# Attention, experts and a gated layer on one core: the order of the last layer's gate passes and weight passes

## The chip, the cores and the metric

One NeuronCore of a Trainium2 chip runs the whole program in one launch. The metric is device time in microseconds, the median of three runs. The output is float32.

## What is computed

Three layers follow each other on 2304 tokens of 512 values.

```python
p_packed = sm_attn(p, k, v)               # 4 batches, 8 heads, 576 tokens, 32 packed queries
x = sm_attn(q, p_packed, p_packed)        # softmax attention, both times
for e in range(4):                        # experts, 512 -> 1024 -> 512, weighted by domain_probs
    out += p[:, e:e + 1] * (np.maximum(x @ w1[e], 0.0) @ w2[e])
h = out @ w_in                            # the last layer, 512 -> 2048
r = np.maximum(h, 0.0)
g = s * (r * r) + b                       # the gate
return g @ w_out                          # 2048 -> 512
```

The change touches only the last layer.

## The kernel before

Every product of the last layer runs on TensorE with each operand split in a high part (rounded for the engine's fast float32 form) and a low part (what the rounding left): three matmuls stand for one. A split is two passes: ACT copies the high part, and DVE (POOL for w_out) subtracts it from the source.

The layer's width of 2048 is cut in four groups g of 512 (NG = 4), the tokens in three pairs tp of two blocks of 384 (T3 = 384, NTP = 3). A **tile** is one (g, tp). Inside a tile both products are 2 x 2 block products done with seven multiplications in place of eight, named 11, 12, s2, s3, s1, s4, 22 (OPS); the s are sums of blocks. A tile's first product is 7 operations k times 2 column blocks j, so 14 **steps** (UP = 14) of six 384-column matmuls (L1053, `m3_mm`). `m3_next` takes the results from PSUM: operations 11, s2, s3 and 22 accumulate in one bank per j ("a"), which is read after each of them, 12, s1 and s4 take a bank of their own ("b"). ACT copies (L1110, L1118, L1112), DVE adds (L1119), and four quarters of h come out: z0 with 12, z3 with s3, z1 with s4, z2 with 22. ORDER says in which order the seven are done.

From group 1 on the gate is five short functions, put on steps by a table (`at(step, fn, ...)`, in the loop over g near the end; `pos` turns a unit of the last layer into a step): `q_relu` (ACT, L1128), `q_gate` (ACT, a square L1133 and a scale with bias L1135), `q_sum` (DVE, the sums s1 to s4 of the gated quarters, L1147) and `q_part` (the split: high pass on ACT L1156, low pass on DVE L1159). The quarters are called 11, 12 for the upper and 21, 22 for the lower values; the upper are z0 and z1 of j = 0, 1, the lower z2 and z3.

The second product (L1191, `m4_next`) has seven operations again, in the order LAST, of 18 matmuls of 256 columns: three row blocks i of 128 tokens with six each. It lags by 18 steps, nine matmuls behind each step's six (`second`). Rows 0 and 2 of an operation share a PSUM bank (o0 or o2, by b), the middle row 1 sits in bank o1, whose two halves serve the operations in turn. After row 1, and again after row 2, DVE adds the bank to the output in SBUF (L1206); TensorE may write a bank again only after that addition has read it. In the last group the finished rows go out by DMA from SP.

Beside a tile, the next group's operands are made. `wop_parts` splits w_in's operand for operation k (ACT L789, DVE L790, two column blocks each), a step apart, during the last tile (tp = 2) of the group before; `wi_sums` (POOL, L774 to L781) forms the block sums in place, `wov_parts` does w_out's (ACT L831, POOL L832) from step 6 of a group's first tile. Operands of x come back from DRAM by SP's DMAs (`xs_load`).

Each engine runs its own queue in order; what stands in front and waits holds everything behind it.

Of the kernel before, what the change touches and what calls it, by code (L numbers as in the profile page):

```python
# [19 lines left out]
def attention_experts_mlp_kernel(  # L20
# [675 lines left out]
    ORDER = ("11", "12", "s2", "s1", "s3", "s4", "22")  # L696
    LAST = ("12", "11", "s2", "s1", "s3", "s4", "22")
# [85 lines left out]
    def wop_parts(g, k):  # L783
        n = g * NK + k
        tag = "w1" if n % 8 < 4 else "w1p"
        t = wop[g, k] = keep.tile([P, NQ, 2, HK * P], F32R, tag=tag, bufs=4, name=f"wop{g}{k}")
        for j in range(NQ):
            src = tw[g * NQ + j][(ORDER if g else OPS)[k]]
            nc.scalar.activation(t[:, j, 0], src, AF.Copy)  # L789
            nc.vector.tensor_tensor(out=t[:, j, 1], in0=src, in1=f32(t[:, j, 0]), op=ALU.subtract)  # L790
# [21 lines left out]
    def wov_sums(g, n):  # L812
# [8 lines left out]
        else:  # L821
            t = tv[g]
            t2, t4 = t["s2"], t["22"] = t["11"], t["12"]
            nc.gpsimd.tensor_tensor(out=t2, in0=t["s4"], in1=t["s1"], op=ALU.subtract)
            nc.gpsimd.tensor_tensor(out=t4, in0=t4, in1=t2, op=ALU.subtract)
# [311 lines left out]
    def q_sum(g, tp, what):  # L1137
# [3 lines left out]
            "s3": ("11", "21", ALU.subtract, "21"), "s4": ("12", "s2", ALU.subtract, "12"),  # L1141
# [39 lines left out]
    def m4_next(g, tp, k, i, n):  # L1181
# [4 lines left out]
        if (bank, "next") not in o_ps:  # L1186
# [7 lines left out]
            start=(n == 0 and i < 2 and (op in ("11", "12") or (op, i) == ("s1", 0))),  # L1194
# [12 lines left out]
        if g == NG - 1 and op in ("s4", "22"):  # L1207
            for j in (1,) if i == 1 else (0, 2):
                r0 = t * T3 + j * P
                nc.sync.dma_start(out=out[r0 : r0 + P], in_=o_sb[t][:, j])  # L1210


    with tc.manual_schedule():
# [291 lines left out]
        for g in range(1, NG):  # L1505
# [4 lines left out]
            for k in range(NK):  # L1510
                at(u0 + 2 * k + 1, wop_parts, g, k)
# [9 lines left out]
            for tp in range(NTP):  # L1521
                i = pos((g * NTP + tp) * UP)
                for j in range(NQ):
                    for d, n in ((3, 0), (9, 3), (11, 1)):
                        at(i + d + j, q_relu, g, tp, j, n)
                    for c in range(2):
                        for n in range(2):
                            at(i + 11 + 2 * c + j + n, q_gate, g, tp, f"{c + 1}{j + 1}", n)
                for n in range(2):
                    for k in range(2):  # L1530
                        at(i + 13 + n, q_part, g, tp, k, n)
                for d, what in ((16, "s1"), (16, "s2"), (18, "s3"), (19, "s4")):
                    at(i + d, q_sum, g, tp, what)
                for k in range(2, NK):
                    for n in range(2):
                        at(i + 13 + 2 * k + n, q_part, g, tp, k, n)
# [45 lines left out]
        def behind(g, tp, *_):  # L1582
            if g == 0:
# [5 lines left out]
                for k in range(NK) for x in range(NS) for n in range(6)  # L1589
# [60 lines left out]
```

## Time and profile before

| what | value |
|---|---|
| median of three runs | 1069.21 us (1068.4 to 1069.44) |
| the profiled execution | 1069.46 us |
| its span (first to last instruction) | 1067.7 us |
| TensorE matmuls (PE) busy | 1046.9 us, 98% |
| VectorE (DVE) busy | 687.2 us, 64% |
| ScalarE (ACT) busy | 542.2 us, 51% |
| GpSimd (POOL) busy | 211.2 us, 20% |
| granted TensorE clock | 0.999 of full speed |

The profile is of one execution; the span is 1.8 us shorter than that execution's time. PE's busy time includes the modelled end of each matmul, so a short wait can hide in it. A row of a group tells the line of the kernel, the engine, the operation, output<-inputs, shapes and count, then the busy time and the mean, then how long the engine stood idle just before such instructions and what ended that.

### The profile page before, as it was taken

The numbers are of one execution on the slowest core, as the hardware profiler recorded it, in microseconds if no ns is written. First come the engines' busy times: TensorE is split into PE (matmuls) and PEld (weight loads), VectorE is DVE, ScalarE is ACT, GpSimd is POOL, SyncE is SP. The second block draws the span as 40 slices with busy tenths as digits, with TensorE's granted clock in tenths as the row PEclk, the third lists the DMA queues.
The fourth block names the chain that finished last, engine by engine and source line by source line (L and its number), as shares of the span: only waits on it lengthen the run. The fifth ranks groups of instructions, "written<-read, shape, count | busy, mean of one in ns | idle before, by whom it ended". The sixth has DMA issues, their size and how long they took to land.

```text
span 1067.7 us, 18211 instructions
## 1 busy us (share of the span) xinstructions
PE 1046.9 (98%) x6701; PEld 924.0 (87%) x6701; DVE 687.2 (64%) x1342; ACT 542.2 (51%) x1165; POOL 211.2 (20%) x222
## 2 busy tenths in 40 slices
PE   8999999999999999999999999999999999999996
PEld 5778888888888888888888888998899899999996
DVE  7885755565664255564365735799536787777776
ACT  3533334533442343443335756766576666766752
POOL 0630330321010321010321122113123142214000
PEclk9999999999999999999999999999999999999999
DMA  9874122986578446584856233347756565565523
GB/s 257 213 127 90 21 91 99 322 223 186 197 250 250 117 121 190 189 250 158 230 141 169 75 104 138 130 193 252 293 178 217 177 207 210 173 210 180 176 89 119
DMA packets 106899, 187.09 MB, mean 175 GB/s; under 512 B 49449, under 2 KB 63785, under 8 KB 106811
## 3 DMA queue, kind: packets, MB, share of 16 engines
q1 hardware_dynamic: 106539, 185.87, 55.9%
q8 instruction: 53, 0.87, 0.3%
q14 instruction: 35, 0.29, 0.1%
q10 hardware_dynamic: 272, 0.07, 0.0%
HBM read 131.11 MB, written 54.79 MB: 174 GB/s over the span
## 4 chain that ended last, share of the span: by engine, by line
PE 80%; ACT 8%; DVE 7%; issue 2%; DMA 2%; SPq 1%; ACTq 0%; DVEq 0%
PE acc L889 35%; PE h L843 19%; PE h L1053 10%; PE on L1191 6%; PE o L1171 5%; ACT z L1133 2%; ACT z L1135 2%; PE pp L625 2%; DVE o_sb L1206 1%; DVE gg L1159 1%; ACT gg L1156 1%; DMA v<-in_v_dram 1%; DVE z L1119 1%; ACT z L1128 1%; DVE wop L790 1%
## 5 line engine op out<-in xcount | busy, mean ns | idle before, releaser
L843 PEld LDWEIGHTS h<-a,w1p 128*128 128x128 f32 x1536 | 229.1, 188 | 26.5 <-issue 5.6
L843 PE MATMUL h<-a,w1p 128*128 128x320 f32 (+1 forms) x1536 | 248.4, 297 | 0.5 <-DVE hl L866 0.4
L866 DVE SCALAR_TENSOR_TENSOR hl<-h,hh 128x256 fp32r<-128x256 f32 x256 | 107.7, 421 | 216.9 <-ACT rest L864 111.0
L864 ACT ACTIVATE hh<-h 128x256 fp32r<-128x256 f32 x256 | 98.8, 386 | 221.5 <-PE h L843 218.6
L1053 PE MATMUL h<-xs,wop 128*128 128x384 f32 x1008 | 203.0, 337 | 0.0
L889 PE MATMUL acc<-w2l,hh 128*128 128x512 f32 x512 | 201.8, 394 | 0.0
L889 PE MATMUL acc<-w2h,hh 128*128 128x512 f32 x512 | 201.3, 393 | 0.0
L889 PE MATMUL acc<-w2h,hl 128*128 128x512 f32 x512 | 200.4, 391 | 0.0
L1053 PEld LDWEIGHTS h<-xs,wop 128*128 128x128 f32 x1008 | 173.0, 188 | 5.0
L1191 PE MATMUL on<-wov,gg 128*128 128x256 f32 x1134 | 157.2, 283 | 11.7 <-DVE o_sb L1206 11.1
L1191 PEld LDWEIGHTS on<-wov,gg 128*128 128x128 f32 x1134 | 148.6, 189 | 17.4 <-DVE o_sb L1206 15.2
L889 PEld LDWEIGHTS acc<-w2h,hl 128*128 128x128 f32 x512 | 96.2, 188 | 22.0
L889 PEld LDWEIGHTS acc<-w2l,hh 128*128 128x128 f32 x512 | 96.4, 188 | 15.0 <-DVE xt L914 0.4
L889 PEld LDWEIGHTS acc<-w2h,hh 128*128 128x128 f32 x512 | 96.3, 188 | 13.2
L1206 DVE TENSOR_TENSOR o_sb<-on,o_sb 128x256 f32<-128x256 f32 x126 | 67.3, 552 | 23.4 <-PE on L1191 22.6
L1171 PE MATMUL o<-wo,gg 128*128 128x512 f32 x216 | 57.2, 395 | 0.0
L688 POOL TENSOR_TENSOR w2l<-w2r,w2h 128x512 fp32r<-128x512 f32 x24 | 31.7, 1329 | 107.2 <-ACT w2h L685 106.4
L1159 DVE TENSOR_TENSOR gg<-z,gg 128x768 fp32r<-128x768 f32 x45 | 47.1, 1064 | 7.9 <-ACT gg L1156 7.9
L1128 ACT ACTIVATE z<-z 128x384 f32<-128x384 f32 x54 | 28.0, 521 | 37.3 <-DVE z L1119 37.1
L1171 PEld LDWEIGHTS o<-wo,gg 128*128 128x128 f32 x216 | 39.9, 188 | 5.9 <-DVE gg L1028 0.2
L633 DVE TENSOR_TENSOR w1o<-pp,w1o 128x512 fp32r<-128x512 f32 x48 | 29.8, 684 | 20.8 <-ACT w1o L632 20.8
L941 ACT ACTIVATE x<-xt 32x384 f32<-32x384 f32 x80 | 41.9, 523 | 1.3
(449 smaller groups left out, 1340.6 us busy)
## 6 DMA issues: line engine op xcount, KB each, us to landing
xs<-xs_dram SPq DMA_DIRECT2D x63, 768.0 KB, 4.2
w1p_dram<-w1o SPq DMA_DIRECT2D x48, 512.0 KB, 4.1
w1p<-w1p_dram SPq DMA_DIRECT2D x192, 128.0 KB, 4.3
xs_dram<-xs SPq DMA_DIRECT2D x21, 768.0 KB, 3.3
w1r<-in_moe_w_dram SPq DMA_DIRECT2D x12, 512.0 KB, 4.4
w2r<-in_moe_w_dram SPq DMA_DIRECT2D x24, 256.0 KB, 5.1
out_dram<-o_sb SPq DMA_DIRECT2D x18, 256.0 KB, 2.3
v<-in_v_dram SPq DMA_DIRECT2D x8, 512.0 KB, 9.1
```

The source lines that it names most:

```text
L688: nc.gpsimd.tensor_tensor(out=lo, in0=raw_t.pop((e, f)), in1=f32(hi), op=ALU.subtract)
L843: nc.tensor.matmul(t[:, : width(bi, hf)], lhsT=w1p_block(e, bi, f, gi, w), rhs=a2[bi][:, x, gi, part(bi, hf)], start=(n == 0), stop=(n == ...
L864: nc.scalar.activation(hi, src, AF.Relu)
L866: nc.vector.scalar_tensor_tensor(out=lo, in0=src, scalar=0.0, in1=f32(hi), op0=ALU.max, op1=ALU.subtract)
L889: nc.tensor.matmul(acc[j], lhsT=x, rhs=w, start=(f == 0 and n == 0), stop=(g == NF - 1 and n == 2),)
L941: nc.scalar.activation(dst[32 * q : 32 * q + 32, a], src[:, q], AF.Copy)
L1053: nc.tensor.matmul(ps, lhsT=w[:, a, col], rhs=x[:, z, m, :], start=(fresh and n == 0), stop=(n == 3 * HK - 1), skip_group_check=chain,)
L1128: nc.scalar.activation(z, z, AF.Relu)
L1159: nc.vector.tensor_tensor(out=t[:, 1], in0=src, in1=f32(t[:, 0]), op=ALU.subtract)
L1171: nc.tensor.matmul(acc, lhsT=lhsT, rhs=w, start=(f == 0 and n == 0), stop=(f == FG - 1 and n == 2),)
L1191: nc.tensor.matmul(ps[:, half], lhsT=gg[g, tp, k][:, x, r, i * P : (i + 1) * P], rhs=wov[g, k][:, w, r, :], start=(n == 0 and i < 2 and (o ...
L1206: nc.vector.tensor_tensor(out=dst, in0=src, in1=dst, op=ALU.add)
```

## The change

In the last layer, for groups 1 to 3:

- ORDER does 22 sixth and s4 seventh, so the lower values z2 and z3 are complete two steps sooner and z1 two steps later. The table moves `q_relu` of z1 by two steps and gates the lower values at steps 11 to 13, the upper at 14 to 16 (before: upper first).
- LAST begins with s1 (the sum of the two lower values), then 11, s2, s4, s3, 22, and ends with 12. Sums and splits are put on steps 14 to 28 in that order; the first split, with 12 and 11 at step 13 before, is at 15 now and each is two steps ahead of its use (before four). s4 gets a buffer of its own, since 12 is needed last. `wov_sums` stores its last block sum over s1.
- `wop_parts` issues the high pass at step 2k and the low pass at 2k + 1 (before both at 2k + 1).
- The second product does row 1 first, then 0, then 2 (before 0, 1, 2); the start flags and the output DMAs follow the new order.

```diff
--- before.py
+++ after.py
@@ -693,8 +693,8 @@
 
     OPS = ("11", "12", "s2", "s3", "s1", "s4", "22")
     NK = len(OPS)
-    ORDER = ("11", "12", "s2", "s1", "s3", "s4", "22")
-    LAST = ("12", "11", "s2", "s1", "s3", "s4", "22")
+    ORDER = ("11", "12", "s2", "s1", "s3", "22", "s4")
+    LAST = ("s1", "11", "s2", "s4", "s3", "22", "12")
     wi_dram = [dram.tile([P, 2, DM], F32, name=f"wi_dram{q}") for q in range(DFF // P // 2)]
     wo_dram = [dram.tile([P, DM], F32, name=f"wo_dram{fb}") for fb in range(DFF // P)]
 
@@ -780,14 +780,20 @@
                 nc.gpsimd.tensor_tensor(out=t2, in0=t["s4"], in1=t["s1"], op=ALU.subtract)
                 nc.gpsimd.tensor_tensor(out=t4, in0=t4, in1=t2, op=ALU.subtract)
 
-    def wop_parts(g, k):
+    def wop_parts(g, k, which=(0, 1)):
         n = g * NK + k
         tag = "w1" if n % 8 < 4 else "w1p"
-        t = wop[g, k] = keep.tile([P, NQ, 2, HK * P], F32R, tag=tag, bufs=4, name=f"wop{g}{k}")
+        if 0 in which:
+            wop[g, k] = keep.tile([P, NQ, 2, HK * P], F32R, tag=tag, bufs=4, name=f"wop{g}{k}")
+        t = wop[g, k]
         for j in range(NQ):
             src = tw[g * NQ + j][(ORDER if g else OPS)[k]]
-            nc.scalar.activation(t[:, j, 0], src, AF.Copy)
-            nc.vector.tensor_tensor(out=t[:, j, 1], in0=src, in1=f32(t[:, j, 0]), op=ALU.subtract)
+            if 0 in which:
+                nc.scalar.activation(t[:, j, 0], src, AF.Copy)
+            if 1 in which:
+                nc.vector.tensor_tensor(
+                    out=t[:, j, 1], in0=src, in1=f32(t[:, j, 0]), op=ALU.subtract
+                )
 
     def wo_tile(fb):
         t = wodd.tile([P, 2, DM], F32R, tag="w1p", bufs=FG, name=f"wo{fb}")
@@ -820,9 +826,9 @@
             tv[g] = {"11": b11, "12": b21, "s1": b12, "s3": t3, "s4": b22}
         else:
             t = tv[g]
-            t2, t4 = t["s2"], t["22"] = t["11"], t["12"]
+            t2, t4 = t["s2"], t["22"] = t["11"], t["s1"]
             nc.gpsimd.tensor_tensor(out=t2, in0=t["s4"], in1=t["s1"], op=ALU.subtract)
-            nc.gpsimd.tensor_tensor(out=t4, in0=t4, in1=t2, op=ALU.subtract)
+            nc.gpsimd.tensor_tensor(out=t4, in0=t["12"], in1=t2, op=ALU.subtract)
 
     def wov_parts(g, k):
         pool, tag = (gb, "wo") if ((g - 1) * NK + k) % 8 < 4 else (wodd, "w1p")
@@ -1138,7 +1144,7 @@
         a = quad[g, tp]
         x, y, op, dst = {
             "s1": ("21", "22", ALU.add, None), "s2": ("s1", "11", ALU.subtract, None),
-            "s3": ("11", "21", ALU.subtract, "21"), "s4": ("12", "s2", ALU.subtract, "12"),
+            "s3": ("11", "21", ALU.subtract, "21"), "s4": ("12", "s2", ALU.subtract, None),
         }[what]
         if dst is None:
             dst = wb.tile([P, HK, T3], F32, tag="sx", bufs=3, name=f"q{what}_{g}{tp}")
@@ -1191,7 +1197,7 @@
         nc.tensor.matmul(
             ps[:, half],
             lhsT=gg[g, tp, k][:, x, r, i * P : (i + 1) * P], rhs=wov[g, k][:, w, r, :],
-            start=(n == 0 and i < 2 and (op in ("11", "12") or (op, i) == ("s1", 0))),
+            start=(n == 0 and i < 2 and (op in ("s1", "12") or (op, i) == ("11", 0))),
             stop=(n == 5), skip_group_check=True,
         )
         if n < 5 or i == 0:
@@ -1204,7 +1210,7 @@
         if i == 1:
             dst = dst[:, 0]
         nc.vector.tensor_tensor(out=dst, in0=src, in1=dst, op=ALU.add)
-        if g == NG - 1 and op in ("s4", "22"):
+        if g == NG - 1 and op in ("22", "12"):
             for j in (1,) if i == 1 else (0, 2):
                 r0 = t * T3 + j * P
                 nc.sync.dma_start(out=out[r0 : r0 + P], in_=o_sb[t][:, j])
@@ -1508,7 +1514,8 @@
                 at(u0 - 5, load_wi, q)
             at(u0 - 2, wi_sums, g, 0)
             for k in range(NK):
-                at(u0 + 2 * k + 1, wop_parts, g, k)
+                for x in range(2):
+                    at(u0 + 2 * k + x, wop_parts, g, k, (x,))
                 if k == 1:
                     at(u0 + 3, wi_sums, g, 1)
                 for tp in range(NTP):
@@ -1521,19 +1528,16 @@
             for tp in range(NTP):
                 i = pos((g * NTP + tp) * UP)
                 for j in range(NQ):
-                    for d, n in ((3, 0), (9, 3), (11, 1)):
+                    for d, n in ((3, 0), (9, 3), (13, 1)):
                         at(i + d + j, q_relu, g, tp, j, n)
                     for c in range(2):
                         for n in range(2):
-                            at(i + 11 + 2 * c + j + n, q_gate, g, tp, f"{c + 1}{j + 1}", n)
-                for n in range(2):
-                    for k in range(2):
-                        at(i + 13 + n, q_part, g, tp, k, n)
-                for d, what in ((16, "s1"), (16, "s2"), (18, "s3"), (19, "s4")):
+                            at(i + 14 - 3 * c + j + n, q_gate, g, tp, f"{c + 1}{j + 1}", n)
+                for d, what in ((14, "s1"), (17, "s2"), (18, "s4"), (20, "s3")):
                     at(i + d, q_sum, g, tp, what)
-                for k in range(2, NK):
+                for k in range(NK):
                     for n in range(2):
-                        at(i + 13 + 2 * k + n, q_part, g, tp, k, n)
+                        at(i + 15 + 2 * k + n, q_part, g, tp, k, n)
 
         wb = wf = wodd = None
         stack_f = ExitStack()
@@ -1586,7 +1590,7 @@
                 ]
             return [
                 (m4_next, g, tp, k, x, n)
-                for k in range(NK) for x in range(NS) for n in range(6)
+                for k in range(NK) for x in (1, 0, 2) for n in range(6)
             ]
 
         def second(count):
```

What the table makes of DVE's queue where the tile (1, 2) ends (818 to 857 us of the trace): names end in g, tp and k, so wop26 is the operand of group 2 for operation 6, gg116 the gate operand of tile (1, 1) for operation 6, o_sb the output, on a bank of the second product. Before:

```order
L1119 TENSOR_TENSOR z120_9211<-h1250_9453,uv0_7683 128x384
L790 TENSOR_TENSOR wop25_9476<-wi4_9087,wop25_9476 128x256
L790 TENSOR_TENSOR wop25_9476<-wi5_9089,wop25_9476 128x256
L1119 TENSOR_TENSOR z121_9237<-h1251_9481,uv1_7719 128x384
L1206 TENSOR_TENSOR o_sb3_8630<-on_1_8988,o_sb3_8630 128x256
L1206 TENSOR_TENSOR o_sb3_8630<-on_2_8981,o_sb3_8630 128x2x256
L1159 TENSOR_TENSOR gg116_9470<-z111_8918,gg116_9470 128x768
L790 TENSOR_TENSOR wop26_9528<-wi4_9087,wop26_9528 128x256
L790 TENSOR_TENSOR wop26_9528<-wi5_9089,wop26_9528 128x256
L1206 TENSOR_TENSOR o_sb3_8630<-on_1_8988,o_sb3_8630 128x256
L1206 TENSOR_TENSOR o_sb3_8630<-on_0_9028,o_sb3_8630 128x2x256
```

and with the change:

```order
L1212 TENSOR_TENSOR o_sb2_8493<-on_2_8987,o_sb2_8493 128x2x256
L1165 TENSOR_TENSOR gg115_9472<-z111_8915,gg115_9472 128x768
L1125 TENSOR_TENSOR z120_9209<-h1260_9502,uv0_7683 128x384
L1212 TENSOR_TENSOR o_sb3_8630<-on_1_8979,o_sb3_8630 128x256
L794 TENSOR_TENSOR wop26_9499<-wi4_9086,wop26_9499 128x256
L794 TENSOR_TENSOR wop26_9499<-wi5_9088,wop26_9499 128x256
L1125 TENSOR_TENSOR z121_9236<-h1261_9528,uv1_7719 128x384
L1212 TENSOR_TENSOR o_sb3_8630<-on_0_9033,o_sb3_8630 128x2x256
L1165 TENSOR_TENSOR gg116_9520<-z111_8915,gg116_9520 128x768
L1153 TENSOR_TENSOR qs1_12_9549<-z120_9209,z121_9236 128x768
L1212 TENSOR_TENSOR o_sb3_8630<-on_1_8979,o_sb3_8630 128x256
```

The low passes of wop26 stood directly in front of two additions whose inputs TensorE had finished; now what stands behind them (z121, then an addition) waits for products that TensorE finishes later.

ACT's queue at the same place, which makes the high parts (wop) that those low passes wait for. Before:

```order
L1135 ACTIVATE z120_9211<-z120_9211,b_sb_80,s_sb_79 128x768
L1128 ACTIVATE z121_9237<-z121_9237 128x384
L1133 ACTIVATE z121_9237<-z121_9237 128x768
L1112 ACTIVATE z120_9211<-h1200_9212 128x384
L1133 ACTIVATE z120_9211<-z120_9211 128x768
L1135 ACTIVATE z121_9237<-z121_9237,b_sb_80,s_sb_79 128x768
L1156 ACTIVATE gg120_9522<-z121_9237 128x768
L1156 ACTIVATE gg121_9524<-z120_9211 128x768
L789 ACTIVATE wop26_9528<-wi4_9087 128x256
L789 ACTIVATE wop26_9528<-wi5_9089 128x256
```

and with the change:

```order
L1118 ACTIVATE z120_9209<-h1200_9210 128x384
L1162 ACTIVATE gg115_9472<-z111_8915 128x768
L1139 ACTIVATE z120_9209<-z120_9209 128x768
L1118 ACTIVATE z121_9236<-h1201_9237 128x384
L1141 ACTIVATE z120_9209<-z120_9209,b_sb_80,s_sb_79 128x768
L1139 ACTIVATE z121_9236<-z121_9236 128x768
L792 ACTIVATE wop26_9499<-wi4_9086 128x256
L792 ACTIVATE wop26_9499<-wi5_9088 128x256
L1162 ACTIVATE gg116_9520<-z111_8915 128x768
L1134 ACTIVATE z120_9209<-z120_9209 128x384
L1141 ACTIVATE z121_9236<-z121_9236,b_sb_80,s_sb_79 128x768
```

The two high passes of wop26 stood behind two splits of the gate (gg120, gg121) at the end of the tile; now they stand behind a square, with one split behind them.

DVE's queue in the tail, from the split of the last operation of tile (3, 1), gg316, on (qs1, qs2 and qs4 are the sums, z320 and z321 the quarters of the last tile). Before:

```order
L1159 TENSOR_TENSOR gg316_11422<-z311_10902,gg316_11422 128x768
L1206 TENSOR_TENSOR o_sb3_8630<-on_1_8988,o_sb3_8630 128x256
L1206 TENSOR_TENSOR o_sb3_8630<-on_0_9028,o_sb3_8630 128x2x256
L1159 TENSOR_TENSOR gg320_11467<-z321_11213,gg320_11467 128x768
L1159 TENSOR_TENSOR gg321_11469<-z320_11192,gg321_11469 128x768
L1206 TENSOR_TENSOR o_sb2_8490<-on_1_8988,o_sb2_8490 128x256
L1206 TENSOR_TENSOR o_sb2_8490<-on_2_8981,o_sb2_8490 128x2x256
L1147 TENSOR_TENSOR qs1_32_11517<-z320_11192,z321_11213 128x768
L1147 TENSOR_TENSOR qs2_32_11519<-qs1_32_11517,z320_11192 128x768
L1206 TENSOR_TENSOR o_sb3_8630<-on_1_8988,o_sb3_8630 128x256
L1206 TENSOR_TENSOR o_sb3_8630<-on_0_9028,o_sb3_8630 128x2x256
L1147 TENSOR_TENSOR z320_11192<-z320_11192 128x768
```

and with the change:

```order
L1165 TENSOR_TENSOR gg316_11468<-z311_10906,gg316_11468 128x768
L1153 TENSOR_TENSOR qs1_32_11493<-z320_11193,z321_11219 128x768
L1212 TENSOR_TENSOR o_sb3_8630<-on_1_8979,o_sb3_8630 128x256
L1212 TENSOR_TENSOR o_sb3_8630<-on_0_9033,o_sb3_8630 128x2x256
L1165 TENSOR_TENSOR gg320_11508<-qs1_32_11493,gg320_11508 128x768
L1212 TENSOR_TENSOR o_sb2_8493<-on_1_8979,o_sb2_8493 128x256
L1153 TENSOR_TENSOR qs2_32_11535<-qs1_32_11493,z320_11193 128x768
L1212 TENSOR_TENSOR o_sb2_8493<-on_2_8987,o_sb2_8493 128x2x256
L1153 TENSOR_TENSOR qs4_32_11551<-z321_11219,qs2_32_11535 128x768
L1165 TENSOR_TENSOR gg321_11537<-z320_11193,gg321_11537 128x768
L1212 TENSOR_TENSOR o_sb5_8885<-on_1_8979,o_sb5_8885 128x256
L1212 TENSOR_TENSOR o_sb5_8885<-on_2_8987,o_sb5_8885 128x2x256
```

Before, two splits, two additions and two sums stand together in front of the addition of gg316's rows (o_sb3); now splits, sums and additions alternate.

## Rows read from the trace of the kernel before

**Rows 1.** Windows by tile: length; busy PE, PEld, DVE, ACT, POOL; clock, DMA, GB/s

```profile
818.60:851.30 32.70, 30.66 (x212) 29.73 (x211) 24.66 (x44) 21.90 (x42) 3.81 (x4) 1.00 0.50 169
851.30:883.10 31.80, 30.08 (x212) 29.57 (x212) 24.76 (x36) 21.21 (x36) 11.09 (x8) 1.00 0.64 207
883.10:914.10 31.00, 30.45 (x213) 29.74 (x212) 23.18 (x34) 21.15 (x35) 8.11 (x7) 1.00 0.61 213
914.10:946.50 32.40, 30.71 (x212) 29.77 (x212) 24.57 (x44) 21.63 (x41) 3.83 (x4) 1.00 0.50 171
946.50:978.40 31.90, 30.21 (x213) 29.72 (x212) 24.67 (x36) 21.31 (x36) 11.07 (x8) 1.00 0.60 206
978.40:1009.30 30.90, 30.45 (x213) 29.75 (x212) 23.08 (x33) 21.12 (x34) 4.58 (x3) 1.00 0.52 180
1009.30:1038.10 28.80, 28.80 (x203) 28.49 (x202) 20.73 (x32) 17.79 (x29) 0.00 (x0) 1.00 0.31 110
1038.10:1063.10 25.00, 21.53 (x172) 20.55 (x171) 19.36 (x30) 9.50 (x12) 0.00 (x0) 1.00 0.22 82
```

**Rows 2.** Timeline of PE, last tile and tail: start us, us, what [idle before it]

```profile
1009.33 1.21 PE L1053 MATMUL h<-xs,wop 128*128 128x384 f32 x6
...
1037.07 1.21 PE L1053 MATMUL h<-xs,wop 128*128 128x384 f32 x6
1038.11 6.46 PE L1191 MATMUL on<-wov,gg 128*128 128x256 f32 x51
1046.02 2.38 PE L1191 MATMUL on<-wov,gg 128*128 128x256 f32 x18 [1.44 <-DVE o_sb L1206]
1049.55 1.70 PE L1191 MATMUL on<-wov,gg 128*128 128x256 f32 x12 [1.15 <-DVE o_sb L1206]
1052.12 10.97 PE L1191 MATMUL on<-wov,gg 128*128 128x256 f32 x90 [0.87 <-DVE o_sb L1206]
```

**Rows 3.** Waits of PE over the span: us in total, times, longest

```profile
PE on L1191 <- DVE o_sb L1206: 11.1, 14, 1.7
```

**Rows 4.** Timeline of DVE where tile (1, 2) has just ended

```profile
853.86 0.76 DVE L790 TENSOR_TENSOR wop<-wi,wop 128x256 fp32r<-128x256 f32 x2 [3.78 <-ACT wop L789]
854.53 1.02 DVE L1206 TENSOR_TENSOR o_sb<-on,o_sb 128x256 f32<-128x256 f32 x2
```

**Rows 5.** Timeline of ACT at the same place

```profile
851.94 1.58 ACT L1156 ACTIVATE gg<-z 128x768 fp32r<-128x768 f32 x2
853.42 0.71 ACT L789 ACTIVATE wop<-wi 128x256 fp32r<-128x256 f32 x2
```

**Rows 6.** Timeline of PE at the same place

```profile
852.41 0.87 PE L1191 MATMUL on<-wov,gg 128*128 128x256 f32 x6
855.00 0.62 PE L1191 MATMUL on<-wov,gg 128*128 128x256 f32 x3 [1.72 <-DVE o_sb L1206]
```

**Rows 7.** Groups of DVE by line, 787.9 to 1063.1: busy us, mean ns, idle before

```profile
L1206 DVE TENSOR_TENSOR o_sb<-on,o_sb 128x256 f32<-128x256 f32 x125 | 66.7, 551 | 23.1 <-PE on L1191 22.3
...
L790 DVE TENSOR_TENSOR wop<-wi,wop 128x256 fp32r<-128x256 f32 x24 | 9.1, 418 | 18.4 <-ACT wop L789 18.4
L1119 DVE TENSOR_TENSOR z<-h,z 128x384 f32<-128x384 f32 x16 | 8.8, 553 | 6.1 <-PE h L1053 6.1
```

**Rows 8.** Timeline of DVE in the tail

```profile
1043.68 0.96 DVE L1147 TENSOR_TENSOR qs<-z,z 128x768 f32<-128x768 f32 x1 [0.94 <-ACT z L1135]
...
1045.55 1.01 DVE L1206 TENSOR_TENSOR o_sb<-on,o_sb 128x256 f32<-128x256 f32 x2
...
1055.15 0.95 DVE L1159 TENSOR_TENSOR gg<-z,gg 128x768 fp32r<-128x768 f32 x1
```

**Rows 9.** Timelines of POOL and DVE where they meet

```profile
879.71 1.30 POOL L832 TENSOR_TENSOR wov<-wv,wov 128x512 fp32r<-128x512 f32 x1 [3.32 <-ACT wov L831]
879.79 2.04 DVE L1159 TENSOR_TENSOR gg<-z,gg 128x768 fp32r<-128x768 f32 x1
```

## The prediction, made before the changed kernel ran

> **What bounds the kernel now.** I read the windows first, cut at the start of each tile of the last layer. A tile is 14 steps; a step is one block of six first products (h) and, from the second group on, nine second products (on) [rows 1]. TensorE is busy in nearly all of the span, so only the time in which it does not issue can be won. How long a tile has to be is read from the last one: its first block of h starts at 1009.33, its last at 1037.07 [rows 2], so 13 steps take 27.74 us, a step 2.134 us, a tile of 14 steps 29.87 us. The six tiles from 818.60 to 1009.30 take 32.70, 31.80, 31.00, 32.40, 31.90 and 30.90 us [rows 1]; less 29.87 each that is 2.83 + 1.93 + 1.13 + 2.53 + 2.03 + 1.03 = 11.5 us of lost time. The tail, 1038.11 to 1063.09, has only second products, 51 + 18 + 12 + 90 = 171 of them [rows 2]. At the pace of the last block, 10.97 / 90 = 0.122 us each, they need 20.8 us; the tail takes 25.0, so 4.2 us are lost there. 11.5 + 4.2 = 15.7 us is all that can be had.
>
> Then who is waited for. The view of waits names one line, DVE's L1206, the additions that empty the banks of the second product [rows 3]. Its 11.1 us are fewer than 15.7, because the modelled end of a matmul covers the first tenths of each wait. And the additions are not slow (0.55 us) [rows 7]; they are queued behind something else.
>
> What stands in front of them differs by place. At 853.86 DVE had sat idle for 3.78 us until ACT's L789 came [rows 4]: L790, the low part of the first product's weights, stood in DVE's queue ahead of two additions and could not start, since ACT reached the matching high part only at 853.42, behind two gate passes [rows 5]. The additions came at 854.53, and TensorE, which had stopped after six of nine matmuls, went on at 855.00 after 1.72 us [rows 6]. From 787.9 to 1063.1 the waits of L790 for L789 sum to 18.4 us [rows 7]. In the tail the block is the gate itself: DVE's first sum waits 0.94 us for ACT's L1135, then two sums run (1043.68 to 1045.6), and only then the addition for which TensorE has waited since 1044.57 [rows 2, 8].
>
> **The change part by part.** No instruction is added or removed: every engine but SP has as many rows as before, and SP's two more are the same output DMAs standing apart. So each term is a wait.
>
> *Weight operands.* The high pass moves from step 2k + 1 to 2k, the low pass stays at 2k + 1. I laid the two queues of the tile at 818.60 out with the new order and the durations of these rows (0.71 us for two high passes [rows 5], 0.76 for two low ones, 1.02 for a pair of additions [rows 4], about 0.95 for a gate pass on DVE [rows 8]); times count from the tile's first h. The seven high passes are done at 1.5, 6.6, 10.4, 12.9, 17.1, 22.0 and 27.5 us; DVE comes to the low passes at 3.0, 7.7, 11.6, 16.2, 19.7, 23.7 and 28.2. None waits; the closest is the last, by 0.7 us. The third high pass is the one that gets a new wait: its source is a difference that POOL makes after DVE's second low pass, and ACT stands about 0.4 us for it (in the 10.4). Nobody else is late by it. This is the wait behind most of the loss in the tiles at 818.60 and 914.10 and, at the seam, in those that follow: 2.83 + 1.93 + 2.53 + 2.03 = 9.3 us.
>
> *Gate order.* The lower values (z2, z3) are complete with the sixth product instead of the seventh, so ACT squares and scales them while the last product still runs, and DVE's four sums and seven low passes are spread one to two a step instead of standing in a cluster. The price is the margin: a low pass is now issued two steps ahead of the matmuls that read it, before four. In the same layout the narrowest low part is ready 2.6 us early (11.2 against 13.8 us), and the narrowest addition frees its bank 0.8 us early (9.5 against 10.3). Beside POOL this shrinks: a gate low pass that met a POOL pass took 2.04 us [rows 9] against 0.95 alone [rows 8]; with two stretched so, 0.3 us is left of the 0.8. So the other two tiles (1.13 + 1.03) lose their wait too, but I keep 1.0 us of the 11.5 for places where 0.3 us is not enough. The ends: 0 kept, or nothing won but the weight tiles, 9.3.
>
> Here a rule of the Trainium skill speaks against the change: "SBUF — State Buffer", section "SBUF: two separate sides", says that a VectorE operation with two SBUF inputs and a GpSimd operation that reads SBUF take a common port pair as an exclusive lock, and the loser waits out the whole instruction. By the row the low pass lost 2.04 - 0.95 = 1.09 us; by the rule it would be up to the POOL pass's whole 1.30. What either makes of the time is rival B.
>
> *Rows of the second product.* The middle row block now comes first of the three. Its bank is shared by both halves of the operations, and TensorE waits for the other half's addition as well. It has as long as before between an addition's input and the next use (12 matmuls); the pair of the same bank gets six more, 0.7 us. In the steady part that only adds margin.
>
> *The tail.* The same layout from 1038.11, with 0.122 us a matmul: TensorE waits 0.2 us for the pair before operation 22 of the last tile but one, 0.65 at its last operation (the addition stands behind a low pass and the first sum), 0.5 for the bank of the first operation of the last tile (12 and s1 use the same one), 0.65 at 11 and 0.55 at s2 (each behind two or three gate passes of 0.95), and 0.2 at the last 22: 2.75 us. Now it is 4.2, so 1.4 is won. Bounds: nothing, or all 4.2.
>
> *At no cost:* the reorder of the products changes which bank is taken when, always three products ahead; s4 takes a third buffer of a ring of three whose earlier reader ended ten steps before; POOL's passes are as many, two with other operands; the output DMAs after the last addition are two as before, so the 4.6 us from 1063.1 to the end stay.
>
> **Sum.** 11.5 - 1.0 + 1.4 = 11.9 us. The profiled execution took 1069.46 us, 0.25 above the median of the runs: 1069.46 - 11.9 = 1057.6, less 0.25 is **1057.3 us**.
>
> **The rivals.**
> A: ACT stays late. The high pass at the tile's end still stands behind a copy, two squares and a scale; if ACT is one step (2.13 us) later than I laid it out, which the 3.78 us of [rows 4] shows to be possible, DVE waits as before at the busiest two or three of seven passes. For it: the margin there is 0.7 us only. Against: ACT is busy 21.9 of 32.70 us in that tile [rows 1]. Half of the 9.3 us stays: 1057.3 + 4.7 = 1062.0.
> B: The halved lead is too short beside POOL. Four of the tiles have POOL busy for 4.6 to 11.1 us [rows 1]; if two low passes in each lose 1.09 us and only 0.3 of it is covered, 4 x 2 x 0.8 = 6.3 us come back, less the 1.0 kept: 1062.6. By the skill's rule it would be 4 x 2 x 1.0 = 8.0 less 1.0, 1064.3. Against: two of them, where no weight pass stood, lost 1.0 and 1.1 us before.
> C: Slower, by a new chain in TensorE's own queue. The accumulated bank goes 11, s2, s3, 22, and 22 follows s3 by two steps now instead of four. Its first matmul must wait until DVE's L1119 (z from h and z) has read s3's value. In my layout that is 1.4 us ahead of need. Were DVE late by the 3.78 us of [rows 4], TensorE would lose 2.4 us a tile, 21.6 in nine tiles: 1057.3 + 21.6 = 1078.9. It decides against the change from 1.4 + 11.9 / 9 = 2.7 us of lateness in every tile. Against it: those 16 additions waited 6.1 us for TensorE and for nobody else [rows 7]; DVE was there first.
> D: The wait only moves, as DVE has too much to do: 24.66 us of a tile [rows 1], 83% of 29.87. Then some 1068.
>
> **How the numbers follow.** My forecast 0.58, A 0.2, B 0.11, D 0.06, C 0.05. About 0.2% (2.1 us) is what a measurement of this kernel tells from no change. Forecast, A and B all lie below 1067.1, so faster is 0.89; D is the same, 0.06; C slower, 0.05. The range reaches down to all 15.7 us won, 1069.2 - 15.7 = 1053.5, and up to A with nothing won in the tail, 1062.0 + 1.4 = 1063.4, say 1063.5.
>
> **What would show it.** In the profile after: the tiles of the last layer at 30 us each, 32 where I am wrong; L790's low pass no longer among DVE's waits for ACT (18.4 us now); TensorE's wait for the additions at some 3 us in total, nearly all in the last 25 us; the tail at 23.6 us. If low passes of the weights still wait for ACT, A holds; if the waits stand where POOL is busy, B; if TensorE's h waits for DVE's L1119, C.

## The result, and the profile after

The changed kernel takes **1055.78 us** (median of 4 runs, 1055.55 to 1056.62), the kernel before 1069.33 beside it (1068.4 to 1069.6): a ratio of 0.9876, 95% interval 0.9859 to 0.9893. That is 13.5 us gained, where 11.9 were forecast; the forecast of 1057.3 lies 1.5 us high and its range holds the time. The profiled execution took 1055.56 us, its span 1053.8. As it turned out, the time was nearly right while one of the reasons was not.

The windows by tile, cut at the first h of each tile as in [rows 1] and with the same columns:

```profile
817.90:847.60 29.70, 29.70 (x213) 29.70 (x212) 25.92 (x47) 22.51 (x44) 3.69 (x4) 1.00 0.54 186
847.60:877.20 29.60, 29.60 (x213) 29.60 (x211) 24.07 (x33) 20.35 (x34) 11.51 (x8) 1.00 0.66 223
877.20:906.90 29.70, 29.70 (x213) 29.70 (x212) 22.45 (x33) 20.64 (x34) 7.77 (x7) 1.00 0.64 222
906.90:936.50 29.60, 29.60 (x211) 29.60 (x211) 25.92 (x47) 22.36 (x44) 3.68 (x4) 1.00 0.55 187
936.50:966.20 29.70, 29.70 (x213) 29.70 (x212) 24.08 (x33) 20.36 (x34) 11.36 (x8) 1.00 0.64 222
966.20:995.90 29.70, 29.70 (x213) 29.70 (x212) 22.09 (x33) 20.58 (x34) 4.30 (x3) 1.00 0.53 187
995.90:1024.40 28.50, 28.50 (x203) 28.50 (x203) 20.31 (x32) 17.53 (x29) 0.00 (x0) 1.00 0.32 111
1024.40:1048.10 23.70, 22.10 (x172) 20.67 (x170) 20.00 (x32) 9.82 (x13) 0.00 (x0) 1.00 0.24 88
```

Every tile now has the same length, whether ACT makes weight operands in it or POOL is at work. The six took 190.7 us (818.60 to 1009.30) and take 178.0 (817.90 to 995.90): 12.7 won. The tail went from 25.0 to 23.7 us, 1.3 won; the last tile gave 0.3 and the way up to the first of these tiles 0.7. Of that 0.7, 0.4 stands ahead of the changed tiles: the last layer begins that much sooner in this trace (at 658.50 instead of 658.88), and over the 14 traces of this document it begins anywhere from 658.5 to 660.5. From the last matmul to the end of the span it was 1067.7 - 1063.09 = 4.6 us and is 1053.8 - 1048.04 = 5.8: 1.15 lost. 12.7 + 1.3 + 0.3 + 0.7 - 1.15 = 13.85, and the spans differ by 13.9.

Of TensorE's waits over the span, that for the additions, beside [rows 3]:

```profile
PE on L1197 <- DVE o_sb L1212: 1.4, 4, 0.5
```

All four stand in the tail, as its timeline shows (beside [rows 2]):

```profile
1023.31 1.21 PE L1059 MATMUL h<-xs,wop 128*128 128x384 f32 x6
1024.35 3.71 PE L1197 MATMUL on<-wov,gg 128*128 128x256 f32 x27
1028.53 3.09 PE L1197 MATMUL on<-wov,gg 128*128 128x256 f32 x24 [0.46 <-DVE o_sb L1212]
1031.77 1.68 PE L1197 MATMUL on<-wov,gg 128*128 128x256 f32 x12 [0.15 <-DVE o_sb L1212]
1033.93 2.38 PE L1197 MATMUL on<-wov,gg 128*128 128x256 f32 x18 [0.48 <-DVE o_sb L1212]
1036.60 11.44 PE L1197 MATMUL on<-wov,gg 128*128 128x256 f32 x90 [0.29 <-DVE o_sb L1212]
```

On DVE, the groups by line from 787.5 to 1048.1 beside [rows 7]:

```profile
L1212 DVE TENSOR_TENSOR o_sb<-on,o_sb 128x256 f32<-128x256 f32 x126 | 69.3, 552 | 43.5 <-PE on L1197 43.4
...
L794 DVE TENSOR_TENSOR wop<-wi,wop 128x256 fp32r<-128x256 f32 x24 | 9.0, 414 | 0.0
L1125 DVE TENSOR_TENSOR z<-h,z 128x384 f32<-128x384 f32 x16 | 8.8, 553 | 3.4 <-PE h L1059 3.2
```

The low passes of the weights (L794) wait for nothing, where L790 waited 18.4 us. The additions cost the same 0.55 us on average (the line mixes two sizes: a middle row takes 0.41 us, the two rows of a bank together 0.69) and now wait for TensorE: DVE is there first.

The chain that ended last, share of the span by engine, of the kernel before:

```profile
PE 80%; ACT 8%; DVE 7%; issue 2%; DMA 2%; SPq 1%; ACTq 0%; DVEq 0%
```

The same of the changed kernel:

```profile
PE 96%; DVE 1%; DMA 1%; SPq 1%; issue 0%; ACT 0%
```

ACT and DVE have all but left the chain. What idle time the profile still shows on TensorE in the last layer is 1.4 us. The tail's 171 matmuls at 0.122 us each would need 20.8 of its 23.7 us, so some 2.9 are still lost there; about half of that shows as idle time, the rest is hidden under modelled ends.

### The profile page after: what moved, and what is told of

Its sections match the earlier page's. It is cut to its first block, busy times and chain, and to the rows that moved or that the text cites. A ratio compares the mean times of both kernels' runs of the same rounds, so it can differ in the third digit from the quotient of the medians.

```text
span 1053.8 us, 18215 instructions
## 1 busy us (share of the span) xinstructions
PE 1041.9 (99%) x6701; PEld 923.8 (88%) x6701; DVE 684.6 (65%) x1342; ACT 539.0 (51%) x1165; POOL 210.8 (20%) x222
## 4 chain that ended last, share of the span: by engine, by line
PE 96%; DVE 1%; DMA 1%; SPq 1%; issue 0%; ACT 0%
PE acc L895 38%; PE h L849 20%; PE h L1059 17%; PE on L1197 12%; PE o L1177 5%; PE pp L625 2%; DMA v<-in_v_dram 1%; PE pw L539 1%; PE pv L345 1%; PE s L417 0%; DVE o_sb L1212 0%; DVE gg L1165 0%; PE warm L1247 0%; PE tr L328 0%; DVE qs L1153 0%; SPq L134 0%
## 5 line engine op out<-in xcount | busy, mean ns | idle before, releaser
L1197 PE MATMUL on<-wov,gg 128*128 128x256 f32 x1134 | 153.9, 282 | 1.5 <-DVE o_sb L1212 1.4
L1212 DVE TENSOR_TENSOR o_sb<-on,o_sb 128x256 f32<-128x256 f32 x126 | 69.3, 552 | 43.5 <-PE on L1197 43.4
L1165 DVE TENSOR_TENSOR gg<-z,gg 128x768 fp32r<-128x768 f32 x36 | 40.9, 1135 | 0.0
```

Of the source, the lines that this page charges most:

```text
L1165: nc.vector.tensor_tensor(out=t[:, 1], in0=src, in1=f32(t[:, 0]), op=ALU.subtract)
L1197: nc.tensor.matmul(ps[:, half], lhsT=gg[g, tp, k][:, x, r, i * P : (i + 1) * P], rhs=wov[g, k][:, w, r, :], start=(n == 0 and i < 2 and (o ...
L1212: nc.vector.tensor_tensor(out=dst, in0=src, in1=dst, op=ALU.add)
```

## The experiments

"Faster" is against the kernel before, run on the same chip with each group of experiments; a ratio stands with its 95% interval. The change has three parts: W (weight passes split, the high one sooner), G (gate and product order) and R (rows 1, 0, 2). The first group of runs takes them apart. In what was expected, theory 1 is the prediction's own: W frees DVE and is most of the gain. Theory 2, its rival, is that G alone does the work; theory 3 came out of the first runs and is told with the fourth.

**W alone**

```
+    def wop_parts(g, k, which=(0, 1)):
...
-                at(u0 + 2 * k + 1, wop_parts, g, k)
+                for x in range(2):
+                    at(u0 + 2 * k + x, wop_parts, g, k, (x,))
```

> The kernel before with one part of the change: high passes of the weight operands at step 2k, low passes at 2k + 1. Theory 1 (the low pass stands in DVE's queue behind a high pass that ACT has not reached): the two weight tiles and the tiles behind them lose nearly all of their 9.3 us, the other tiles and the tail stay: 1060 to 1062 us. Theory 2 (the cluster of sums and low passes of the old gate order holds the additions up, the weights are only caught in it): little comes of it, 1066 to 1069 us.

Measured: 1060.53 us (1060.13 to 1061.88), 0.9922 [0.9907, 0.9937]: 9.2 us faster, as theory 1 wanted (9.3). The six tiles take 181.7 us in its trace instead of 190.7, so the gain stands where it was expected.

**G alone** (the new ORDER and LAST, q_gate, q_sum, q_part; rows 0, 1, 2 and the joint weight pass as before)

```
-    ORDER = ("11", "12", "s2", "s1", "s3", "s4", "22")
-    LAST = ("12", "11", "s2", "s1", "s3", "s4", "22")
+    ORDER = ("11", "12", "s2", "s1", "s3", "22", "s4")
+    LAST = ("s1", "11", "s2", "s4", "s3", "22", "12")
...
```

> The kernel with the new gate order alone: old weight passes (both at step 2k + 1), old row order. Theory 1: the two regular tiles (2.2 us) and part of the tail are won, the weight tiles only in part, as ACT is less crowded at the tile's end: 1062 to 1066 us. Theory 2: nearly all of the gain is here, 1056 to 1058 us.

Measured: 1066.07 us (10 runs, 1064.28 to 1068.63), 0.9972 [0.9962, 0.9981]: 3.7 us faster, at the slow end of what theory 1 gave. The new order alone does not do the work of the weight split: DVE's low passes still wait 12.5 us for ACT in its trace.

**R alone**

```
-                for k in range(NK) for x in range(NS) for n in range(6)
+                for k in range(NK) for x in (1, 0, 2) for n in range(6)
```

> The kernel before with the row order 1, 0, 2 alone. Both theories: the pair of the same bank has six matmuls (0.7 us) more, which matters only where a pair is the last to be read: 1067.5 to 1069.5 us.

Measured: 1063.92 us (1062.99 to 1065.2), 0.9953 [0.9936, 0.9969]: 5.8 us faster. Every theory so far had priced this at next to nothing. The longest of DVE's waits for ACT in its trace (us in total, times, longest):

```profile
DVE wop L790 <- ACT wop L789: 17.5, 10, 3.8
```

And TensorE's waits in the same trace:

```profile
PE on L1191 <- DVE o_sb L1206: 8.8, 12, 1.5
```

DVE stands behind ACT nearly as long as before (20.2 us over that stretch), and TensorE still loses less: the rows give the additions more time to be late in. The waits shown on TensorE fall by 2.3 us alone (from 11.1); the rest of the 5.8 had been hidden.

**W and G, without R** (the changed kernel with rows 0, 1, 2 again: the line above undone)

> The changed kernel with the old row order 0, 1, 2. Theory 1: the steady tiles stay without a wait; in the tail the same bank's pairs (11 then s2, s3 then 22, 12 then s1) have 0.7 us less, so up to 0.7 us at each of three to four places: 1056 to 1058.5 us. If the row order is worth nothing: 1055.8 us.

Measured: 1062.19 us (1061.75 to 1063.55), 0.9938 [0.9923, 0.9953]: 6.4 us slower than the changed kernel, outside the 1056 to 1058.5 that theory 1 gave. No low pass waits for ACT in it. It is also 1.7 us slower than W alone, but the traces put only 0.8 of that in the changed tiles (the tail and the last tile lose 1.3, the six tiles win 0.5); for the rest its last layer began 1.0 us later. So with W in place and the old rows, the gate order wins nothing. TensorE's timeline in its last tile, then in its tail:

```profile
1015.66 1.21 PE L1059 MATMUL h<-xs,wop 128*128 128x384 f32 x6
1016.71 1.23 PE L1197 MATMUL on<-wov,gg 128*128 128x256 f32 x9
1017.78 1.21 PE L1059 MATMUL h<-xs,wop 128*128 128x384 f32 x6
1019.07 1.30 PE L1197 MATMUL on<-wov,gg 128*128 128x256 f32 x9
1020.21 1.21 PE L1059 MATMUL h<-xs,wop 128*128 128x384 f32 x6
...
1031.82 4.50 PE L1197 MATMUL on<-wov,gg 128*128 128x256 f32 x36 [0.87 <-DVE o_sb L1212]
1037.75 4.51 PE L1197 MATMUL on<-wov,gg 128*128 128x256 f32 x36 [1.43 <-ACT gg L1162]
1043.66 6.70 PE L1197 MATMUL on<-wov,gg 128*128 128x256 f32 x54 [1.41 <-DVE o_sb L1212]
1051.24 4.50 PE L1197 MATMUL on<-wov,gg 128*128 128x256 f32 x36 [0.88 <-DVE o_sb L1212]
```

The step from 1015.66 takes 2.12 us, the one from 1017.78 takes 2.43, and no idle time is shown in it: the modelled end of the block of h (1017.78 + 1.21 = 1018.99) covers it. Only the start of the next block tells: 1.29 us after its h instead of 1.05. From the starts of h, this tile (from 1000.73) has three long steps, the first 2.19, the fifth 2.19 and the ninth this 2.43; the other ten are 2.11 to 2.13. The tile before it has the same three and takes 30.1 us (970.63 to 1000.73), where the changed kernel's take 29.6 to 29.7. The tail takes 26.0 us (1029.72 to 1055.74), the changed kernel's 23.7. (About 1.3 of the 6.4 us stand before the last layer in the two traces, at 659.83 against 658.50.)

From this run and the next comes **theory 3**: what counts is the time between the matmul that fills a bank and the next that writes it. With rows 0, 1, 2, row 1 is full at matmul 12 of 18 and the next operation wants that bank at 25: 12 matmuls of 0.118 us, and one block of h (1.05 us), 2.5 us. With 1, 0, 2 it is full at 6 and wanted at 19: the same 12 matmuls, but two blocks of h, 3.5 us. Where two operations in turn use the same bank for rows 0 and 2, the time was one block of h, 1.05 us; now six matmuls more, 1.76 us. What has to fit into it is the addition of that bank, 0.69 us, and where the middle row's addition is late too, both, 1.01 us. G's order has three such pairs of operations a tile (11 to s2, s3 to 22, 12 to the next s1), the order before one (11 to s2). Those are the three long steps. They are not equally long, and DVE's timeline at the ninth step says why:

```profile
1017.43 0.56 DVE L1125 TENSOR_TENSOR uv<-h,uv 128x384 f32<-128x384 f32 x1 [0.80 <-ACT z L1124]
1017.91 1.01 DVE L1212 TENSOR_TENSOR o_sb<-on,o_sb 128x256 f32<-128x256 f32 x2
```

Here the middle row's addition stands behind an addition for h that waits 0.80 us for ACT, so both additions come after it, and the step loses 0.32 us. At the first step the middle row was added earlier (at 1000.34), only the 0.69 us of the other bank are left, and the step loses 0.08.

**G and R, weight passes joint as before**

```
-                for x in range(2):
-                    at(u0 + 2 * k + x, wop_parts, g, k, (x,))
+                at(u0 + 2 * k + 1, wop_parts, g, k)
```

> The changed kernel with the weight passes put back (both at step 2k + 1). Theory 1: DVE waits for L792 again in the two weight tiles, and the additions behind it: 1060 to 1063 us. Theory 2: no change, 1056 us.

Measured: 1056.89 us (1055.04 to 1057.52), 0.9874 [0.9853, 0.9895], not to be told from the changed kernel. Theory 1 falls: W is not needed once G and R are there. Its waits of DVE for ACT's high pass:

```profile
DVE wop L794 <- ACT wop L792: 9.3, 8, 1.5
```

And all of TensorE's waits shown in the last layer:

```profile
PE on L1197 <- DVE o_sb L1212: 1.4, 4, 0.5
```

DVE still waits for ACT eight times, 9.3 us, and TensorE waits for exactly what it waits for without that; the six tiles take 178.1 us instead of 177.9. Here the longest such wait is 1.5 us, where R alone left 3.8, and R's longer time covers it.

**Both passes a step sooner**

```
-                for x in range(2):
-                    at(u0 + 2 * k + x, wop_parts, g, k, (x,))
+                at(u0 + 2 * k, wop_parts, g, k)
```

> The changed kernel with both weight passes a step sooner (both at 2k). Theory 1: it is the step between them that counts; the low pass stands right behind the high one again, so DVE waits for ACT as with the passes put back: 1059 to 1063 us. Rival: it is the earlier high pass that counts, 1056 us.

Measured: 1055.70 us (1055.54 to 1055.99), 0.9866 [0.9847, 0.9885]. That the low pass has to stand a step behind the high one falls too: in this trace DVE never waits for ACT's high pass in the tiles of the change, so the earlier high pass is enough. The time could not have shown it, since G and R cover such waits anyway.

**POOL's low pass of the second weights done twice**

```
         nc.scalar.activation(hi, src, AF.Copy)
-        nc.gpsimd.tensor_tensor(out=lo, in0=src, in1=f32(hi), op=ALU.subtract)
+        for _ in range(2):
+            nc.gpsimd.tensor_tensor(out=lo, in0=src, in1=f32(hi), op=ALU.subtract)
```

> The changed kernel with each POOL pass over the second product's weights (the low parts, 21 of them) done twice, the second time to the same values, so that POOL takes the shared way from DVE twice as long. If the halved lead of the gate's low passes is ample beside POOL (my layout: 0.3 us at the narrowest with two passes stretched): 1055.8 to 1058 us. If it is as short as rival B has it: 1060 us or more.

Measured: 1056.59 us (1054.55 to 1057.04), 0.987 [0.9844, 0.9896]: no difference. POOL was busy 245.7 us instead of 210.8 and DVE, with the same 1342 instructions, 694.4 instead of 684.6. DVE is slowed, 9.8 us in all, and TensorE waits the same four times, 1.4 us, as far as waits are shown. The starts of h show a little more: one step each of three tiles with POOL at work takes 2.41 to 2.42 us instead of 2.13 or 2.11, and the six tiles take 178.6 us instead of 177.9. That is far from the 5.3 us of rival B (6.3 less 1.0), even with twice POOL's low passes: rival B falls.

**Output DMAs at the end from two queues**

```
-                nc.sync.dma_start(out=out[r0 : r0 + P], in_=o_sb[t][:, j])
+                eng = nc.scalar if tp == NTP - 1 and op == "12" and j < 2 else nc.sync
+                eng.dma_start(out=out[r0 : r0 + P], in_=o_sb[t][:, j])
```

> The changed kernel with two of the last three output DMAs issued from ACT's queue, which is idle by then. The changed kernel takes 6.0 us from its last matmul to its end, the one before 4.6, with the last three DMAs issued from SP one after the other. If it is SP's queue that holds them up: 0.5 to 1.0 us less, 1054.8 to 1055.3 us. If the landing of the bytes sets the end: no change, 1055.8 us.

Measured: 1055.70 us (1055.08 to 1056.07), 0.9865 [0.9845, 0.9884]: nothing gained. From the last matmul (1049.13) to the end of the span (1054.3) 5.2 us. (The expectation's 6.0 us for the changed kernel is 5.8 by its trace.) Since that time differs between executions, as the last section shows, one trace does not tell whether SP's queue or the landing of the bytes sets it.

**W and R, the old gate order**

> The kernel before with the weight passes split over two steps and the row order 1, 0, 2; the gate order stays old. Theory 3, formed after the first runs (what counts is the time from the matmuls that fill a bank to the next that need it; the row order adds a block of h, 1.05 us, to it): the old gate's lateness in the steady tiles is below 1.05 us, so they fall to 29.7 us each, and only the tail stays longer: 1056.5 to 1058 us. Rival (the gate order has a part of its own in the steady tiles): 1060 us or more.

Measured: 1058.02 us (1057.59 to 1060.41), 0.9892 [0.9863, 0.992], the time that theory 3 gave, but not quite in its place. Not all tiles fall to 29.7 us: the tiles (2, 1) and (3, 1) take 30.8 and 30.7, with one step of 3.24 and 3.14. So the old gate order does have a part of its own in the steady tiles, 2.1 us in two steps, since there an addition is later than R's longer time can cover. DVE and TensorE at the first of them:

```profile
885.59 2.05 DVE L1153 TENSOR_TENSOR qs<-qs,z 128x768 f32<-128x768 f32 x1
887.56 0.55 DVE L1125 TENSOR_TENSOR z<-h,uv 128x384 f32<-128x384 f32 x1
888.03 0.41 DVE L1212 TENSOR_TENSOR o_sb<-on,o_sb 128x256 f32<-128x256 f32 x1
888.58 1.31 PE L1197 MATMUL on<-wov,gg 128*128 128x256 f32 x9 [0.88 <-DVE o_sb L1212]
```

A sum of the gate, 2.05 us long beside POOL, stands in front of the addition. With that all eight combinations are there. The second row is the time in one trace each from the start of tile (1, 1) to the last matmul, which leaves out what differs before the last layer and after the last matmul (us):

| | none | W | G | R | W+G | W+R | G+R | all |
|---|---|---|---|---|---|---|---|---|
| median time | 1069.3 | 1060.5 | 1066.1 | 1063.9 | 1062.2 | 1058.0 | 1056.9 | 1055.8 |
| tile (1, 1) to last matmul | 275.2 | 266.1 | 270.9 | 269.2 | 266.9 | 263.4 | 260.6 | 260.5 |

By the medians W is worth 8.8 by itself, G 3.2 and R 5.4; added last W is worth 1.1, G 2.2 and R 6.4. The last values of W and G are not told from nothing by the intervals. The traces' second row gives 9.1, 4.3 and 5.9 alone, and 0.2, 2.9 and 6.4 last. Three parts that sum to 17.4 by themselves give 13.5 together (in the traces 19.3 and 14.7).

**Another LAST, one same-bank pair a tile (s3 to 22) instead of three; old rows**

```
-    LAST = ("s1", "11", "s2", "s4", "s3", "22", "12")
+    LAST = ("11", "s1", "s2", "s4", "s3", "22", "12")
...
-                for k in range(NK) for x in (1, 0, 2) for n in range(6)
+                for k in range(NK) for x in range(NS) for n in range(6)
```

> The changed kernel with the old row order 0, 1, 2 and another order of the second product, 11, s1, s2, s4, s3, 22, 12, in which one operation follows another on the same bank (22 after s3) where the changed kernel has three (s2 after 11, 22 after s3, s1 after 12). Theory 3: the steps 4 and 8 of a tile fall from 2.18 and 2.43 to 2.11 us, and the tail loses two of its long waits: 1058.5 to 1060.5 us, against 1062.2 with the old rows and the changed order. Rival (the row order counts for the middle row alone): 1062 us as before.

Measured: 1057.85 us (1056.36 to 1057.98), 0.9881 [0.9859, 0.9903]: 4.3 us faster than W and G with the changed kernel's order and the same rows. The steps that were long are 2.11 to 2.13 again but for one of 2.17 to 2.19 a tile, and the tail is 24.2 us (1024.85 to 1049.06) instead of 26.0. So the loss of W and G against the changed kernel comes mostly from the order in which the banks follow each other. Theory 3 holds for these steps, though it had expected 0.7 to 2.7 us more time than this.

**The same LAST with rows 1, 0, 2**

> The changed kernel with the order 11, s1, s2, s4, s3, 22, 12 and the new rows 1, 0, 2. Theory 3: the steady tiles have nothing left to win, the tail has one pair on the same bank fewer at two places (0.07 and 0.15 us) but its first operation waits for an upper value: 1055 to 1056.5 us.

Measured: 1055.39 us (1054.85 to 1056.27), 0.9862 [0.984, 0.9884].

**Rows 0, 2, 1**

```
-                for k in range(NK) for x in (1, 0, 2) for n in range(6)
+                for k in range(NK) for x in (0, 2, 1) for n in range(6)
```

> The changed kernel with the rows in the order 0, 2, 1: the pair comes first and the middle row last. From filling to need the pair has 6 matmuls and a block of h, as with 1, 0, 2, and the middle row 12 matmuls and two blocks of h, as with 1, 0, 2. Theory 3: 1055.3 to 1056.5 us. Rival (the middle row has to be first): towards the 1062.2 of the old order.

Measured: 1055.25 us (1054.7 to 1055.93), 0.986 [0.9839, 0.9882]. The middle row need not come first. With 0, 2, 1 the pair is full at matmul 12 and, in the same bank, wanted at 19: six matmuls and a block of h, the same 1.76 us; row 1 is full at 18 and wanted at 31: 12 matmuls and two blocks of h, the same 3.5 us. Equal times by the count, equal times on the chip. None of these three is told from the changed kernel by its interval; nothing that was run beats it.

## Why the prediction came out as it did

**The steady tiles: right in the place, 2.2 us short in the size.** 10.5 us of the 11.5 were to be won, 12.7 were. The 1.0 us that I kept back for the narrow leads was not lost. The other 1.2 us is the reference tile: I took 2.134 us a step from the last tile of the kernel before as free of waits. It was not. TensorE's timeline of the kernel before, in that tile:

```profile
1024.12 1.21 PE L1053 MATMUL h<-xs,wop 128*128 128x384 f32 x6
1025.16 1.23 PE L1191 MATMUL on<-wov,gg 128*128 128x256 f32 x9
1026.23 1.21 PE L1053 MATMUL h<-xs,wop 128*128 128x384 f32 x6
1027.43 1.33 PE L1191 MATMUL on<-wov,gg 128*128 128x256 f32 x9
1028.60 1.21 PE L1053 MATMUL h<-xs,wop 128*128 128x384 f32 x6
```

From 1026.23 to 1028.60 it is 2.37 us, from 1024.12 to 1026.23 2.11; no idle time is shown. This is the order's one same-bank pair (11 to s2), and DVE's two additions come late, behind one for h that waited for ACT:

```profile
1025.89 0.56 DVE L1119 TENSOR_TENSOR uv<-h,uv 128x384 f32<-128x384 f32 x1 [1.56 <-ACT z L1118]
1026.36 1.01 DVE L1206 TENSOR_TENSOR o_sb<-on,o_sb 128x256 f32<-128x256 f32 x2
```

The same place of the changed kernel, the eighth and ninth step of the tile:

```profile
1010.62 1.21 PE L1059 MATMUL h<-xs,wop 128*128 128x384 f32 x6
1011.66 1.23 PE L1197 MATMUL on<-wov,gg 128*128 128x256 f32 x9
1012.73 1.21 PE L1059 MATMUL h<-xs,wop 128*128 128x384 f32 x6
1013.78 1.23 PE L1197 MATMUL on<-wov,gg 128*128 128x256 f32 x9
1014.84 1.21 PE L1059 MATMUL h<-xs,wop 128*128 128x384 f32 x6
```

2.11 and 2.11. My tile of 29.87 us was 0.2 too long; the real one is 178.0 / 6 = 29.67, and six times 0.2 is the 1.2.

**The weight term: its size right alone, not the one cause.** 9.3 us were put to the low pass that waits for ACT, and W alone gives 8.8 to 9.2. But in the changed kernel it is worth 1.1 at most, which the runs do not tell from nothing, since G and R together remove the same loss in another way: G shortens DVE's wait, R covers what is left of it. The step "this is the wait behind most of the loss" was true of the kernel before and did not mean that only its removal would help.

**The gate term: right.** 1.13 + 1.03 = 2.2 us were put to the two tiles without weight passes. W and R without G lose 2.1 us in just these two (30.8 and 30.7 us).

**The rows: the step that failed.** "In the steady part that only adds margin", with "as long as before" for the middle row, counted matmuls of the second product and left out the blocks of h between them. Counted in time, the middle row gets 3.5 us instead of 2.5. Priced at nothing, R is worth 5.4 us alone and 6.4 last. And "the pair of the same bank gets six more, 0.7 us" was taken for mere margin, while G needs it: three same-bank pairs a tile where there was one. Without R the change gives 7.1 us (1069.3 - 1062.2), not 11.9. The sum came out near the time because R was part of the change and covered what W and G as priced would have left; that much of the agreement is luck.

**The tail: held.** 23.6 us forecast, 23.7 measured; the waits stand where the layout had them. TensorE's four shown waits are 0.46, 0.15, 0.48 and 0.29 (forecast 0.65, 0.5, 0.65 and 0.55, and two of 0.2 that the trace does not show as idle). They are shorter by 0.2 to 0.35 each, but part of each is again covered by modelled ends: 27 matmuls to 1028.53 took 4.18 us, 1.0 more than 27 x 0.118, of which 0.46 is shown.

**The end: not held.** "The 4.6 us from 1063.1 to the end stay" became 5.8 in the profiled execution. See below. This loss of 1.15 and the 2.2 that the tiles gave above the forecast offset each other in part.

**The rivals.** A (ACT late): no low pass of these weights waits for ACT. B (POOL): no wait is shown where POOL is busy, nor with POOL's low passes doubled. Here a rule was weighed, that of the Trainium skill's "SBUF — State Buffer", section "SBUF: two separate sides": a lock between VectorE and GpSimd. With POOL's passes doubled DVE's busy time did grow, 9.8 us for 34.9 us more of POOL, so the trace agrees that DVE loses time beside POOL; whether a pass waits out a whole instruction these sums do not tell. The kernel's time does not show it: the six tiles lost 0.7 us of the 9.8, and the rest was time that DVE had to spare. C (h behind s3's reader): L1125 waited 3.2 us for TensorE, and TensorE's h for nobody. D (DVE full): DVE waits 43.4 us for TensorE in the last layer where it was 22.3 [rows 7].

## What to carry to other kernels

Price a reordering by the time from the instruction that fills a buffer to the next that wants it, and count in everything that the engine does between, not the operation's own instructions alone. Look for such places in the distance between the starts of blocks that repeat, because idle time can be hidden under modelled ends: 0.08 to 0.3 us a step was. Where several parts remove the same loss, run each alone and each left out: a part that is worth 9 us alone was worth 1 or less in company, and one that seemed free carried 6.

## What was not expected of the hardware

The end of the program has two lengths. From TensorE's last matmul to the end of the span it is 4.5 to 4.6 us in the kernel before and in eight of the experiments' traces, and 5.2 to 6.2 in the changed kernel, with both passes sooner, with G and R, with the DMAs on two queues and with the other LAST and old rows. The kernel with POOL's passes doubled issues its output DMAs exactly as the changed one does and has 4.5 (1054.3 - 1049.77), so the order alone does not set it. SP's timeline of two of the six output DMAs of the changed kernel:

```profile
1046.68 1.77 SPq L1216 DMA_DIRECT2D out_dram<-o_sb  x2
```

The same with POOL's passes doubled:

```profile
1048.41 0.81 SPq L1217 DMA_DIRECT2D out_dram<-o_sb  x2
```

One thing goes with the long end in all the traces. A DMA queue that the profile lists as "instruction" moves 16 KB at that moment; from 1046 to 1049 in the changed kernel:

```profile
q8 instruction: 1, 0.02, 3.5%
```

All five traces with a long end have such a transfer between 1.7 us before the last matmul's end and 3.0 after it. The nine with a short end have none from 11 us before the last matmul to the end of the span. In four of the five an issue of an output DMA that begins 0.97 us before the last matmul's end takes 0.92 to 1.38 us, where in the other traces that have one there it takes 0.42 or 0.43. In the fifth (G and R) the transfer comes after the issues, and the last bytes of the output move 4.7 us after the last matmul instead of 3.1. No run moved that transfer, so that it is the cause is not shown. Issuing two of the DMAs from ACT did not change the time. Only one execution of each kernel was traced, so how often a kernel has the long end is open too.
